# First group's attention by pairs of heads, with all scaling on VectorE, and the rows of sums written later

## The chip, the cores and the metric

The kernel runs on one core of one Trainium2 chip. The time is the device time of an execution in microseconds; 725.45 is the median of three runs (725.28 to 726.31). The engines are PE (matrix products), DVE (VectorE), ACT (ScalarE), POOL (GpSimd) and SP (SyncE, which issues most of the loads here); each works through its own instructions in a fixed order.

## What is computed

An attention with a forgetting bias, then two MLPs in a row, all in fp32:

```python
scores = q @ k.T / sqrt(D)                       # B=2, H=8, S=576, D=64
cum = cumsum(maximum(s, 0), -1)
bias = minimum(-(cum[..., :, None] - cum[..., None, :]), 0)
scores = where(causal, -1e9, scores + bias)
attn = exp(scores - max) ; attn = attn / (sum(attn) + 1e-9)
x = (attn @ v)                                   # 1152 tokens x 512
g = elu(x @ w_in) ; x = g @ w_out                # 512 -> 2048 -> 512
p = probs / (sum(probs) + 1e-9)                  # 4 experts, all of them for every token
out = sum_e p[:, e] * (relu(x @ w1[e]) @ w2[e])  # 512 -> 1024 -> 512
```

## The kernel before

The 1152 tokens are taken in three groups (256, 448, 448). Each group goes through attention, layer 1 (the ELU MLP, 16 units of 128 hidden columns, `layer1` at L648) and layer 2 (the experts, 32 units). The attention of the second group runs in pieces between the products of the first group's MLPs (`Background`, L583); the third group's does so in the second's. Only the first group's attention, `attention_first` (L236), has the core to itself, and it is what the change touches.

The weights of layer 1 come as 64-bit words, 512 KB for a half unit, and are decoded on the chip: two passes on ACT (L146, L148) and two on DVE (L149, L151) for a half (`decode_halves`, L131); each finished unit is also written back (`w_dec`, L154, on POOL's queue) for the later groups. The coded halves lie in tiles that have another use later: wu, gt (3), yh, yl, raw (3), xa (3), ox (3), and around again. A tile is refilled by SP (L127) once its last half has been decoded: the three xa halves are refilled together when the third one's L151 is done, and so for ox. SP works in order, so whatever waits there holds up what is behind: after the refills come the loads of the second group's q, k and v (L370, L372, into a tile named pt; L392 and further) and the weights of layer 2 (`fetch`, L93).

`DEC` says how many halves are decoded at four places within `attention_first`, and `AHEAD` how many are to be decoded at each unit of layer 1: 2n + 8 in `advance` (L573).

`attention_first` as it stands: the products of q and k of all heads into six PSUM banks (L277), then the bias for all of them (L283, L285; the sums enter as high and low parts, `cump` and `cumm`, L262 and L263), then the reductions with the mask on DVE (L295) and the exps on ACT (L297), bank by bank. `normalise` (L299) works on four heads at a time: the first query chunk's 128 columns are scaled on DVE (L305), the second's 256 on ACT (L304). Then three transposes a head (L312), a copy to SBUF (L313), the values (L320) and a copy into `xf` (L322), which layer 1 reads. A unit of layer 1 has its up products (L676), exp and its second pass on ACT (L680, L683), gt on DVE (L684) and its down products (L663).

`cum_sums` (L188) forms the sums along the sequence. `cum_parts` (L194) writes what the later groups read: two rows of ones and, twice, the sums' high part (ACT, L202) and low part (DVE, L203) through one tile named rows, from ACT's own queue (L199, L205), into `rows_d` in HBM. As there is one rows tile, ACT's second L202 waits until the first write has landed. The second group's first item reads `rows_d` into qb and kl (L424, L425).

Of the kernel before, what the change touches and what calls it, by code (L numbers as in the profile page):

```python
# [45 lines left out]
DEC = [2, 5, 8, 10]  # L46
AHEAD = 8
# [4 lines left out]
def tile_kernel(ctx, tc, qT, kT, v, s, w64, w, probs, out):  # L52
# [26 lines left out]
    def ps_att():  # L79
        return ps("att", 2)  # L80
# [155 lines left out]
    def attention_first(x):  # L236
# [23 lines left out]
        for t, sign in ((parts, 1.0), (less, -1.0)):  # L260
# [7 lines left out]
        banks = [(range(0, H, 2), 0, "acc0"), (range(1, H, 2), 0, "acc1"),  # L268
                 ((0, 2), 1, "acc2"), ((1, 3), 1, "acc3"), ((4, 6), 1, "up"), ((5, 7), 1, "up")]
        scores = []  # L270
        for heads, i, tag in banks:
            d0, d1 = 128 * i, 128 * i + 128
            o = ps(tag, 2 if tag == "up" else 1)[:, :len(heads) * d1]
            scores.append(o.rearrange("p (h k) -> p h k", k=d1))
            for n_, h in enumerate(heads):
                r = slice(64 * (h % 2), 64 * (h % 2) + 64)
                PE.matmul(scores[-1][:, n_], qkv[r, 0, h // 2, d0:d1], qkv[r, 1, h // 2, 0:d1],  # L277
                          start=n_ == 0, stop=False, skip_group_check=True)
        for (heads, i, tag), o in zip(banks, scores):
            d0, d1 = 128 * i, 128 * i + 128  # L280
            for n_, h in enumerate(heads):
                one = ones[:, h:h + 1]
                PE.matmul(o[:, n_], one.to_broadcast([80, 128]), parts[:, 0:d1],  # L283
                          start=False, stop=False, skip_group_check=True)
                PE.matmul(o[:, n_], less[:, d0:d1], one.to_broadcast([80, d1]),  # L285
                          start=False, stop=n_ == len(heads) - 1, skip_group_check=True)
        cum_parts()

        def probabilities(bank):
            heads, i, _ = banks[bank]  # L290
            d0, d1 = 128 * i, 128 * i + 128
            for n_, h in enumerate(heads):
                p = pp[h][:, d0:d0 + d1]
                nm = sb([128, 1], "nm", 8)
                DVE.tensor_tensor_reduce(p, scores[bank][:, n_], mask[:, S - d1:], -1.0 / SC,  # L295
                                         3.0e38, ALU.add, ALU.min, nm)
                ACT.activation(p, p, AF.Exp, bias=nm, scale=-1.0, accum_out=sm[:, i, h:h + 1])  # L297

        def normalise(h0):  # L299
            r = sm[:, :, h0:h0 + 4]  # L300
# [7 lines left out]
        def transposes(h):  # L308
            pt = ps_att()
            for m in range(3):  # L310
                ms = slice(128 * m, 128 * m + 128)
                PE.transpose(pt[:, ms], pp[h][:, ms], ident)  # L312
            ACT.activation(ptt[:, h], pt[:, :384], AF.Copy)  # L313

        def values(hp, tag):
            o = ps(tag, 1)
# [5 lines left out]
            ACT.activation(x[:, hp], o[:, :n], AF.Copy)  # L322

        probabilities(0)
        probabilities(1)
        decode_halves(DEC[0])
        probabilities(2)
        probabilities(3)
        normalise(0)
        decode_halves(DEC[1])  # L330
        probabilities(4)
        probabilities(5)
        for h in range(4):
            transposes(h)
        normalise(4)
        values(0, "acc0")
        values(1, "acc1")
        decode_halves(DEC[2])
        for h in range(4, 8):
            transposes(h)  # L340
        decode_halves(DEC[3])
        values(2, "acc2")
        values(3, "acc3")
# [361 lines left out]
    attention_first(x_first)  # L705
    cum_columns(0, 4)
    cum_columns(1, 4)
# [17 lines left out]
    yacc = layer1(0, x_first, background)  # L725
# [321 lines left out]
```

## Time and profile before

| | |
|---|---|
| median of three runs | 725.45 us |
| the profiled execution | 726.64 us |
| its span, first to last instruction | 724.8 us |
| PE busy | 693.3 us, 96% of the span |
| DVE busy | 559.1 us, 77% |
| ACT busy | 371.7 us, 51% |
| mean granted PE clock | 0.985 of full speed |

All times below are from the span's start. A row of the timeline has the start, the time from its first to its last end, the engine, the line, the operation with the tile written, an arrow, and the tiles read; in brackets stands how long the engine had been idle and what released it. A row with an engine's name and q (SPq, ACTq) is an instruction that issues a DMA, not the transfer itself.

### The profile page before, as it was taken

The numbers are of one execution on the slowest core, as the hardware profiler recorded it, in microseconds if no ns is written. First come the engines' busy times: TensorE is split into PE (matmuls) and PEld (weight loads), VectorE is DVE, ScalarE is ACT, GpSimd is POOL, SyncE is SP. The second block draws the span as 40 slices with busy tenths as digits, with TensorE's granted clock in tenths as the row PEclk, the third lists the DMA queues.
The fourth block names the chain that finished last, engine by engine and source line by source line (L and its number), as shares of the span: only waits on it lengthen the run. The fifth ranks groups of instructions, "written<-read, shape, count | busy, mean of one in ns | idle before, by whom it ended". The sixth has DMA issues, their size and how long they took to land.

```text
span 724.8 us, 10238 instructions
## 1 busy us (share of the span) xinstructions
PE 693.3 (96%) x3626; PEld 591.7 (82%) x3626; DVE 559.1 (77%) x1142; ACT 371.7 (51%) x777; POOL 13.6 (2%) x33
## 2 busy tenths in 40 slices
PE   5489789999999999999999999999999999999997
PEld 4378678888878888778899988888888888888886
DVE  4678659988875998886795549988888887887765
ACT  3978658776765878666744333222222222332320
POOL 2011000000000000000000000000000000000000
PEclk9599999999999999999999999999999999999999
DMA  8769994667556453441552000111111111111002
GB/s 325 301 237 368 327 319 160 207 198 216 167 188 203 166 158 108 145 141 59 213 222 88 30 0 1 59 58 59 59 58 59 59 58 59 58 59 59 0 1 101
DMA packets 41954, 96.98 MB, mean 134 GB/s; under 512 B 5200, under 2 KB 18704, under 8 KB 41904
## 3 DMA queue, kind: packets, MB, share of 16 engines
q1 hardware_dynamic: 39440, 87.69, 36.5%
q0 software_dynamic: 2304, 8.39, 2.9%
q8 instruction: 28, 0.46, 0.3%
q10 hardware_dynamic: 160, 0.26, 0.1%
q14 instruction: 22, 0.18, 0.1%
HBM read 85.32 MB, written 11.01 MB: 133 GB/s over the span
## 4 chain that ended last, share of the span: by engine, by line
PE 87%; ACT 4%; DMA 3%; DVE 3%; SPq 2%; issue 1%; DVEq 0%; ACTq 0%
PE acc L562 38%; PE up L562 16%; PE att L882 11%; PE up L882 8%; PE att L517 3%; PE att L490 3%; PE acc L663 2%; PE up L676 2%; PE att L445 1%; PE att L438 1%; SPq L370 1%; PE att L440 1%; DMA wu<-in_w 1%; DMA raw<-in_w 1%; DMA q<-in_qT 1%
## 5 line engine op out<-in xcount | busy, mean ns | idle before, releaser
L562 PE MATMUL acc<-w,h 128*128 128x512 f32 x672 | 172.0, 392 | 0.0
L562 PEld LDWEIGHTS acc<-w,h 128*128 128x128 f32 x672 | 126.1, 188 | 23.0 <-ACT h L892 0.2
L83 DVE TENSOR_TENSOR wu<-raw,wu 128x1024 fp32r<-128x1024 f32 x64 | 78.2, 1222 | 22.9 <-ACT wu L99 21.7
L562 PE MATMUL acc<-gt,wu 128*128 128x448 f32 x384 | 88.6, 373 | 0.0
L630 DVE SCALAR_TENSOR_TENSOR ox<-acc,pr,ox 128x512 f32<-128x512 f32 x105 | 78.6, 748 | 10.7 <-PE acc L562 8.6
L892 ACT ACTIVATE h<-c 128x448 fp32r<-128x448 f32 x48 | 27.4, 574 | 114.7 <-DVE c L898 114.7
L99 ACT ACTIVATE wu<-raw 128x1024 fp32r<-128x1024 f32 x64 | 67.5, 1055 | 22.4 <-PE acc L562 16.5
L562 PEld LDWEIGHTS acc<-gt,wu 128*128 128x128 f32 x384 | 70.1, 188 | 8.7 <-issue 2.6
L882 PE MATMUL att<-S,top 128*128 128x448 f32 x288 | 66.3, 365 | 0.0
L882 PEld LDWEIGHTS att<-S,top 128*128 128x128 f32 x288 | 54.0, 188 | 6.7 <-issue 0.2
L562 PE MATMUL acc<-wu,gt 128*128 128x512 f32 x192 | 56.4, 409 | 0.0
L562 PE MATMUL up<-yh,wu 128*128 128x256 f32 x256 | 52.6, 287 | 0.0
L893 DVE SCALAR_TENSOR_TENSOR h<-c,h 128x448 fp32r<-128x448 f32 x48 | 29.9, 624 | 18.7 <-ACT h L892 18.7
L882 PE MATMUL up<-x2a,top 128*128 128x448 f32 x192 | 44.2, 366 | 0.0
L562 PEld LDWEIGHTS up<-yh,wu 128*128 128x128 f32 x256 | 41.9, 190 | 2.7 <-issue 1.7
L562 PE MATMUL up<-xa,wu 128*128 128x448 f32 x192 | 43.6, 371 | 0.0
L562 PE MATMUL up<-ox,wu 128*128 128x448 f32 x192 | 42.1, 368 | 0.7 <-DVE e L688 0.7
L480 ACT ACTIVATE p<-p,nm 128x384 f32<-128x384 f32 (+4 forms) x56 | 34.5, 617 | 13.6 <-DVE nm L475 13.4
L680 ACT ACTIVATE e<-up 128x448 f32<-128x448 f32 (+1 forms) x48 | 23.5, 490 | 33.7 <-PE up L562 31.7
L882 PEld LDWEIGHTS up<-x2a,top 128*128 128x128 f32 x192 | 35.9, 188 | 4.8 <-ACT p L907 0.5
L562 PEld LDWEIGHTS up<-ox,wu 128*128 128x128 f32 x192 | 36.0, 188 | 4.6 <-DVE e L688 1.1
L892 ACT ACTIVATE h<-up 128x448 fp32r<-128x448 f32 x16 | 8.8, 547 | 58.1 <-PE up L882 58.1
(186 smaller groups left out, 1217.8 us busy)
## 6 DMA issues: line engine op xcount, KB each, us to landing
raw<-in_w SPq DMA_DIRECT2D x41, 512.0 KB
raw<-w_dec SPq DMA_DIRECT2D x32, 512.0 KB
raw<-in_w SPq DMA_DIRECT2D x16, 1024.0 KB
w_dec<-wu POOLq DMA_DIRECT2D x16, 512.0 KB, 6.7
k<-in_kT SPq DMA_DIRECT2D x16, 288.0 KB
xa<-in_w SPq DMA_DIRECT2D x6, 512.0 KB
ox<-in_w SPq DMA_DIRECT2D x6, 512.0 KB
cbp<-cum_d SPq DMA_DIRECT2D x16, 144.0 KB
```

Of the source, the lines that this page charges most:

```text
L83: DVE.tensor_tensor(out=lo, in0=x, in1=hi.bitcast(F32), op=ALU.subtract)
L99: ACT.activation(t[:, 0], x, AF.Copy)
L480: ACT.activation(p, p, AF.Exp, bias=nm, scale=-1.0, accum_out=sm)
L490: PE.transpose(pt[:cb[c + 1] - cb[c], m, :], p[:, cb[c]:cb[c + 1]], ident)
L517: PE.matmul(o[64 * j:64 * j + 64, qs:nq], job["v"][:n, c, 64 * j:64 * j + 64], job["pt"][:n, j, c, qs:nq], start=c == 0, stop=c == n_c - 1)
L562: PE.matmul(o, a[m], b[n], start=first and i == 0, stop=last and i == 2)
L630: DVE.scalar_tensor_tensor(out=o_sb, in0=o, scalar=pr[:, i, e:e + 1], in1=o_sb, op0=ALU.mult, op1=ALU.add)
L663: PE.matmul(o, t[:, 512 + 128 * c:640 + 128 * c], gt, start=k == 0, stop=k == NAB - 1)
L680: ACT.activation(e, o, AF.Exp)
L882: PE.matmul(bank, tops[q][:, m, op, cs], x[:, n, c], start=first and c + i == 0, stop=c == 1 and i == 2, skip_group_check=True)
L892: ACT.activation(h[:, 0, u, cs], c, AF.Relu)
L893: DVE.scalar_tensor_tensor(out=h[:, 1, u, cs], in0=c, scalar=0.0, in1=h[:, 0, u, cs].bitcast(F32), op0=ALU.max, op1=ALU.subtract)
```

## The change

In the first group's attention:

- The loads of q and k are split into two chunk pairs each, four DMAs in place of two; the first coded half, then v, then the other halves follow. `cum_sums` is written behind them.
- PE makes twelve 128x128 products whose result nothing reads (`keep_warm`), ahead of the first product of q and k.
- The work goes by pairs of heads: products and bias of one pair, both query chunks of a head in one bank, then reductions and exps, scaling, transposes and values of that pair, with the next pair's steps in between.
- `normalise` makes all sixteen scalings on DVE; ACT has none.
- `DEC` and `AHEAD` are smaller: four halves are decoded within the attention instead of ten, and 2n + 6 by unit n.

`cum_parts`, with the write of `cum_d`, and `cum_columns` move from the attention into a hook after unit k = 3 of layer 1.

```diff
-DEC = [2, 5, 8, 10]
-AHEAD = 8
+DEC = [1, 2, 3, 4]
+AHEAD = 6
...
     def cum_sums():
-        SP.dma_start(out=s_sb, in_=s)
         ACT.activation(s_sb, s_sb, AF.Relu, scale=SC)
         DVE.tensor_tensor_scan(cum, s_sb, s_sb, 0.0, ALU.add, ALU.bypass)
+    def cum_parts():
+
         ACT.dma_start(out=cum_d, in_=cum)
-
-    def cum_parts():
-
         one = sb([B * H, S], "bias", 2)
...
-        cum_sums()
-        SP.dma_start(out=qkv[:, 0], in_=qT[0, :, 0:n].rearrange("(c p) n -> p c n", p=128))
-        SP.dma_start(out=qkv[:, 1], in_=kT[0, :, 0:n].rearrange("(c p) n -> p c n", p=128))
-        fetch_halves(2)
+        SP.dma_start(out=s_sb, in_=s)
+        for c in (0, 2):
+            for i, t in enumerate((qT, kT)):
+                SP.dma_start(out=qkv[:, i, c:c + 2], in_=t[0, 128 * c:128 * c + 256, 0:n]
+                             .rearrange("(c p) n -> p c n", p=128))
+        fetch_halves(1)
...
+        cum_sums()
...
+        chunks = [(0, 128), (128, 256)]
+        banks = {}
+
+        def scores(hp):
+            for j in range(2):
+                h = 2 * hp + j
+                banks[h] = ps(f"acc{h % 4}", 1) if h < 4 or h > 5 else ps("up", 2)
+            for d0, d1 in chunks:
+                for j in range(2):
+                    r = slice(64 * j, 64 * j + 64)
+                    PE.matmul(banks[2 * hp + j][:, d0:d0 + d1], qkv[r, 0, hp, d0:d1],
+                              qkv[r, 1, hp, 0:d1], start=d0 == 0, stop=False,
+                              skip_group_check=True)
...
-            for h in range(h0, h0 + 4):
-                ACT.activation(pp[h][:, 128:], pp[h][:, 128:], AF.Copy, scale=sm[:, 1, h:h + 1])
-                DVE.tensor_scalar(pp[h][:, :128], pp[h][:, :128], sm[:, 0, h:h + 1], None,
-                                  op0=ALU.mult)
...
+            for h in (2 * hp, 2 * hp + 1):
+                for i, (d0, d1) in enumerate(chunks):
+                    p = pp[h][:, d0:d0 + d1]
+                    scaled = DVE.tensor_scalar(p, p, sm[:, i, h:h + 1], None, op0=ALU.mult)
+            return scaled
...
+        def keep_warm(products):
+
+
+            o = ps_att()[:, :128]
+            for _ in range(products):
+                last = PE.matmul(o, ident, ident, start=True, stop=True)
+            return last
+
+        with tc.issue_after(keep_warm(12).ins):
+            for hp in range(3):
+                scores(hp)
         probabilities(0)
+        decode_halves(DEC[0])
+        scores(3)
         probabilities(1)
-        decode_halves(DEC[0])
+        normalise(0)
+        transposes(0)
         probabilities(2)
...
+    def sums_hook(k):
+        if k == 3:
+            with tc.issue_after(after[0].ins), tc.issue_after(after[1].ins):
+                cum_parts()
+            cum_columns(0, 4)
+            cum_columns(1, 4)
+
+    yacc = layer1(0, x_first, background, sums_hook)
```

How this moves the instructions, at three places. First DVE, at the start of the attention; z is half a decoded half, k_, acc_ and sm_ are the probabilities, the banks and the sums, and "ISA" rows of L295 or L299 are the reductions. Before:

```order
L203 SCALAR_TENSOR_TENSOR rows<-cum,rows 16x576
L263 SCALAR_TENSOR_TENSOR cump<-cum,cump 16x256
L263 SCALAR_TENSOR_TENSOR cumm<-cum,cumm 16x256
L203 SCALAR_TENSOR_TENSOR rows<-cum,rows 16x576
L149 SCALAR_TENSOR_TENSOR wu<-wu,z_251 128x512
L151 SCALAR_TENSOR_TENSOR wu<-wu 128x512
L295 ISA k_137,nm<-acc_154,mask 128x128
L295 ISA nm 128x1
```

and now:

```order
L264 SCALAR_TENSOR_TENSOR cump<-cum,cump 16x256
L264 SCALAR_TENSOR_TENSOR cumm<-cum,cumm 16x256
L299 ISA k_138,nm<-acc_168,mask 128x128
L299 ISA nm 128x1
L299 ISA k_138,nm<-acc_168,mask 128x256
```

The low halves of the rows (L203) and the first decoded half stood ahead of the first reduction; now the first reduction follows `cumm` directly.

Second SP, at the first refills of xa and ox; the names after "waits" are counters of landed DMAs and of the engines. Before:

```order
L127 DMA raw<-in_w 128x1024 [waits DMAHW3_49,DVE_49,Activation_49]
L127 DMA xa<-in_w 128x1024 [waits DMAHW4_49,DVE_49,Activation_49]
L127 DMA xa<-in_w 128x1024 [waits DMAHW5_49]
L127 DMA xa<-in_w 128x1024 [waits DMAHW6_49]
L127 DMA ox<-in_w 128x1024 [waits DMAHW7_49,DVE_49,Activation_49]
L127 DMA ox<-in_w 128x1024 [waits DMAHW0_49]
```

and now, from the last raw refill:

```order
L127 DMA raw<-in_w 128x1024 [waits DMAHW7_49,DVE_49,Activation_49]
L127 DMA xa<-in_w 128x1024 [waits DMAHW1_49,DMAHW0_49,DMAHW2_49,DVE_49,Activation_49]
L127 DMA xa<-in_w 128x1024 [waits DMAHW2_49]
L127 DMA xa<-in_w 128x1024 [waits DMAHW3_49]
L444 DMA kl<-rows_d 4x128 [waits DMAHW6_49,DMAHW5_49,DMAHW0_49]
L444 DMA kl<-rows_d 4x128
L443 DMA qb<-rows_d 4x128 [waits DMAHW7_49,DMAHW4_49]
L127 DMA ox<-in_w 128x1024 [waits DVE_49,Activation_49]
L127 DMA ox<-in_w 128x1024 [waits DMAHW1_49]
```

The ox refill followed the xa refill; now the reads of `rows_d` for the second group's first item (kl, kl, qb) stand between them, and qb waits for DMAHW4, which the second rows write on ACT's queue counts up.

Third ACT and DVE, at the new place of the rows. ACT now, from the first of the two copies to the pass behind the second (before, both stood ahead of the attention's exps):

```order
L200 ACTIVATE rows<-cum 16x576
L699 ACTIVATE e<-up 128x256 [waits PE_49]
L148 ACTIVATE z_531<-xa 128x512 [waits DVE_49]
L702 ACTIVATE e<-e 128x256 [waits Activation_49]
L146 ACTIVATE wu<-xa 128x512
L203 DMA rows_d<-rows 16x1152 [waits DMAHW0_49,DVE_49]
L146 ACTIVATE wu<-ox 128x512 [waits DMAHW3_49]
L148 ACTIVATE z_541<-ox 128x512
L699 ACTIVATE e<-up 128x256 [waits PE_49]
L148 ACTIVATE z_560<-ox 128x512 [waits DMAHW4_49,DVE_49]
L200 ACTIVATE rows<-cum 16x576 [waits DMAHW0_49]
L702 ACTIVATE e<-e 128x256 [waits Activation_49]
```

The second copy (L200) waits for DMAHW0, the landing of the first write (L203), and the second pass of a unit's e (L702) is behind it. DVE now, around the same unit:

```order
L151 SCALAR_TENSOR_TENSOR wu<-xa,wu 128x512 x2
L201 SCALAR_TENSOR_TENSOR rows<-cum,rows 16x576
L703 SCALAR_TENSOR_TENSOR gt<-up,e 128x256
L149 SCALAR_TENSOR_TENSOR wu<-wu,z_531 128x512
L151 SCALAR_TENSOR_TENSOR wu<-xa,wu 128x512
L149 SCALAR_TENSOR_TENSOR wu<-wu,z_541 128x512
L151 SCALAR_TENSOR_TENSOR wu<-ox,wu 128x512
L201 SCALAR_TENSOR_TENSOR rows<-cum,rows 16x576
L703 SCALAR_TENSOR_TENSOR gt<-up,e 128x256
```

Before, the third xa half (the last of these three L151 with xa) stood ahead of the gt of the fifth unit:

```order
L151 SCALAR_TENSOR_TENSOR wu<-xa,wu 128x512
L149 SCALAR_TENSOR_TENSOR wu<-wu,z_506 128x512
L151 SCALAR_TENSOR_TENSOR wu<-ox,wu 128x512
L684 SCALAR_TENSOR_TENSOR gt<-up,e 128x256
L149 SCALAR_TENSOR_TENSOR wu<-wu,z_496 128x512
L151 SCALAR_TENSOR_TENSOR wu<-xa,wu 128x512
L149 SCALAR_TENSOR_TENSOR wu<-wu,z_532 128x512
L151 SCALAR_TENSOR_TENSOR wu<-ox,wu 128x512
L684 SCALAR_TENSOR_TENSOR gt<-up,e 128x256
```

Its place is now behind that gt (the first of the two L703 in the rows of the change).

## Rows read from the trace of the kernel before

**Rows 1.** The page: busy time of each engine, and the chain by engine.
```profile
PE 693.3 (96%) x3626; PEld 591.7 (82%) x3626; DVE 559.1 (77%) x1142; ACT 371.7 (51%) x777; POOL 13.6 (2%) x33
...
PE 87%; ACT 4%; DMA 3%; DVE 3%; SPq 2%; issue 1%; DVEq 0%; ACTq 0%
```

**Rows 2.** Windows: length, busy us (PE, PEld, DVE, ACT, POOL), clock, DMA share, GB/s.
```profile
25.00:30.00 5.00, 0.92 (x5) 0.52 (x5) 3.90 (x9) 5.00 (x16) 1.16 (x2) 0.50 1.01 361
45.00:50.00 5.00, 5.00 (x25) 4.41 (x24) 2.47 (x4) 3.00 (x6) 0.53 (x1) 1.00 0.57 227
65.00:70.00 5.00, 5.00 (x25) 4.41 (x24) 4.32 (x9) 4.41 (x9) 0.53 (x1) 1.00 1.03 418
80.00:90.00 10.00, 7.57 (x27) 6.39 (x28) 7.30 (x15) 8.55 (x21) 1.06 (x2) 0.83 1.08 298
100.00:110.00 10.00, 9.10 (x53) 7.77 (x54) 7.56 (x27) 7.42 (x22) 0.00 (x0) 1.00 0.89 260
```

**Rows 3.** Timeline of PE: up products of the third, twelfth, thirteenth unit.
```profile
43.88 1.99 PE L676 MATMUL up<-xf,wu 128*128 128x256 f32 x8 [1.55 <-DVE gt L684]
...
75.06 1.89 PE L676 MATMUL up<-xf,wu 128*128 128x256 f32 x8
...
82.43 3.68 PE L676 MATMUL up<-xf,wu 128*128 128x256 f32 x8 [3.76 <-DVE gt L684]
```

**Rows 4.** Timeline: SP's refills, DVE's gt of the fifth unit, ACT's qb.
```profile
53.14 1.28 SPq L127 DMA_DIRECT2D xa<-in_w  x3
...
55.00 0.42 DVE L684 SCALAR_TENSOR_TENSOR gt<-up,e 128x256 f32<-128x256 f32 x1
...
56.81 1.32 SPq L127 DMA_DIRECT2D ox<-in_w  x3
...
80.84 0.31 ACT L429 ACTIVATE qb<-pt 64x128 fp32r<-64x128 f32 x1 [5.21 <-DMA pt<-in_qT]
```

**Rows 5.** Timeline of ACT and DVE from the first half to the first reduction.
```profile
8.43 0.67 ACT L148 ACTIVATE z<-wu 128x512 int32<-128x512 uint32 x1 [2.73 <-DMA wu<-in_w]
...
9.77 0.41 DVE L263 SCALAR_TENSOR_TENSOR cumm<-cum,cumm 16x256 fp32r<-16x256 f32 x1
...
13.16 0.68 ACT L202 ACTIVATE rows<-cum 16x576 fp32r<-16x576 f32 x1 [3.46 <-DMA rows_d<-rows]
...
13.87 0.74 DVE L203 SCALAR_TENSOR_TENSOR rows<-cum,rows 16x576 fp32r<-16x576 f32 x1 [3.69 <-ACT rows L202]
...
15.72 0.69 DVE L151 SCALAR_TENSOR_TENSOR wu<-wu 128x512 int32<-128x512 int32 x1
16.33 0.28 DVE L295 CUSTOM_DVE_ANT_0 k<-acc,mask 128x128 f32<-128x128 f32 x1
```

**Rows 6.** Groups of ACT by line and form, 10 to 60 us.
```profile
L313 ACT ACTIVATE pt<-att 128x384 f32<-128x384 f32 x8 | 3.6, 507 | 0.0
...
L297 ACT ACTIVATE k<-k,nm 128x256 f32<-128x256 f32 x6 | 3.0, 493 | 0.0
...
L304 ACT ACTIVATE k<-k,sm 128x256 f32<-128x256 f32 x6 | 2.6, 502 | 0.0
...
L297 ACT ACTIVATE k<-k,nm 128x128 f32<-128x128 f32 x6 | 2.3, 388 | 1.7 <-DVE nm L295 1.7
...
L322 ACT ACTIVATE xf<-acc 128x256 f32<-128x256 f32 x4 | 1.5, 419 | 0.0
```

**Rows 7.** Chain in order of time: the first rows write; the first raw weights.
```profile
8.43 4.70 DMA rows_d<-rows
...
86.50 5.80 DMA raw<-in_w
```

**Rows 8.** Timeline of the start: the load of s and its reader.
```profile
0.75 0.40 SPq L189 DMA_DIRECT2D bias<-in_s  x1
...
2.53 0.68 ACT L190 ACTIVATE bias<-bias 16x576 f32<-16x576 f32 x1 [0.50 <-DMA bias<-in_s]
```

**Rows 9.** The page, DMA issues: the write-backs of decoded weights.
```profile
w_dec<-wu POOLq DMA_DIRECT2D x16, 512.0 KB, 6.7
```

More of the change, by code (lines that the diff above doesn't have):

```diff
@@ L264, in attention_first @@
                                      in1=t[:B * H].bitcast(F32), op0=ALU.mult, op1=ALU.subtract)
[L268 to L278, printed above, removed]
@@ L279, in attention_first @@
-        for (heads, i, tag), o in zip(banks, scores):
-            d0, d1 = 128 * i, 128 * i + 128
-            for n_, h in enumerate(heads):
-                one = ones[:, h:h + 1]
[L283 to L297, printed above, removed]
@@ L299, in normalise @@
-        def normalise(h0):
-            r = sm[:, :, h0:h0 + 4]
+        chunks = [(0, 128), (128, 256)]
[10 more added lines that the diff above has]
+                              skip_group_check=True)
+            for j in range(2):
+                h = 2 * hp + j
+                one = ones[:, h:h + 1]
+                for d0, d1 in chunks:
+                    o = banks[h][:, d0:d0 + d1]
+                    PE.matmul(o, one.to_broadcast([80, 128]), parts[:, 0:d1],
+                              start=False, stop=False, skip_group_check=True)
+                    PE.matmul(o, less[:, d0:d1], one.to_broadcast([80, d1]),
+                              start=False, stop=d0 > 0, skip_group_check=True)
@@ new lines, in probabilities @@
+        def probabilities(hp):
+            for j in range(2):
+                h = 2 * hp + j
+                for i, (d0, d1) in enumerate(chunks):
+                    p = pp[h][:, d0:d0 + d1]
+                    nm = sb([128, 1], "nm", 8)
+                    DVE.tensor_tensor_reduce(p, banks[h][:, d0:d0 + d1], mask[:, S - d1:],
+                                             -1.0 / SC, 3.0e38, ALU.add, ALU.min, nm)
+                    ACT.activation(p, p, AF.Exp, bias=nm, scale=-1.0, accum_out=sm[:, i, h:h + 1])
@@ L301, in normalise @@
+        def normalise(hp):
+            r = sm[:, :, 2 * hp:2 * hp + 2]
             DVE.tensor_scalar(r, r, 1e-9, None, op0=ALU.add)
             DVE.reciprocal(r, r)
-            for h in range(h0, h0 + 4):
-                ACT.activation(pp[h][:, 128:], pp[h][:, 128:], AF.Copy, scale=sm[:, 1, h:h + 1])
-                DVE.tensor_scalar(pp[h][:, :128], pp[h][:, :128], sm[:, 0, h:h + 1], None,
-                                  op0=ALU.mult)
[L308 to L313, printed above, removed]
@@ L315, in values, with transposes @@
-        def values(hp, tag):
-            o = ps(tag, 1)
+            for h in (2 * hp, 2 * hp + 1):
+                for i, (d0, d1) in enumerate(chunks):
+                    p = pp[h][:, d0:d0 + d1]
+                    scaled = DVE.tensor_scalar(p, p, sm[:, i, h:h + 1], None, op0=ALU.mult)
+            return scaled
+        def transposes(hp):
+            for h in (2 * hp, 2 * hp + 1):
+                pt = ps_att()
+                for m in range(3):
+                    ms = slice(128 * m, 128 * m + 128)
+                    PE.transpose(pt[:, ms], pp[h][:, ms], ident)
+                ACT.activation(ptt[:, h], pt[:, :384], AF.Copy)
@@ L317, in values @@
+        def values(hp):
+            o = ps(f"acc{(hp + 2) % 4}", 1)
             for c, q0 in ((0, 0), (1, 128)):
@@ L321, in values @@
                               ptt[:, h, 256 * c:256 + 128 * c], start=c == 0, stop=c == 1)
-            ACT.activation(x[:, hp], o[:, :n], AF.Copy)
+            return ACT.activation(x[:, hp], o[:, :n], AF.Copy)
+        def keep_warm(products):
[6 more added lines that the diff above has]
+                scores(hp)
         probabilities(0)
+        decode_halves(DEC[0])
+        scores(3)
         probabilities(1)
-        decode_halves(DEC[0])
+        normalise(0)
+        transposes(0)
         probabilities(2)
+        normalise(1)
+        transposes(1)
+        values(0)
+        decode_halves(DEC[1])
         probabilities(3)
[L329 to L337, printed above, removed]
+        normalise(2)
+        transposes(2)
+        values(1)
         decode_halves(DEC[2])
-        for h in range(4, 8):
-            transposes(h)
+        last = [normalise(3)]
+        transposes(3)
+        values(2)
+        last.append(values(3))
         decode_halves(DEC[3])
-        values(2, "acc2")
-        values(3, "acc3")
+        return last
     def attention_parts(g, x):
@@ L704, in tile_kernel @@
     x_first = sb([128, NCC, GROUPS[0][1]], "xf", 1)
-    attention_first(x_first)
-    cum_columns(0, 4)
-    cum_columns(1, 4)
+    after = attention_first(x_first)
     xs = [None, None, None]
```

1 line of the change is left out of this document (removed).

## Prediction

> **What bounds the kernel now.** The page first: PE is busy for 693.3 us, 96% of the span, and 87% of the chain of waits is PE [rows 1]. So only stretches where PE stands still can give anything. The windows find them: 0.92 of 5 us in 25 to 30, then 7.57 of 10 in 80 to 90 and 9.10 of 10 in 100 to 110 [rows 2]; afterwards PE is the bound. There are thus two holes: the first group's attention, and the end of its layer 1. A gain in the first reaches the end only if it is still there after the second.
>
> The first hole is ACT and DVE work. The third up product, the first after which PE runs on without a break, starts at 43.88, and the twelfth at 75.06: nine steps of 3.46 us [rows 3]. The second hole is a wait for data: ACT stands 5.21 us at the qb copy until pt<-in_qT has landed at 80.84, and the thirteenth up product starts at 82.43, after 3.76 us of PE idle and at half pace, 3.68 us for what takes 1.89 [rows 3, 4]. The clock of that stretch is 0.83 [rows 2]. Those transfers come late because the stream of transfers is full: 418 GB/s from 65 to 70 us [rows 2]. SP started refilling at 53.14, when the third xa half had been decoded, and sent the ox refill at 56.81 [rows 4]. So the question is less when the attention ends than when SP starts this stream.
>
> **The front, part by part.** (1) DVE's first reduction starts at 16.33, though its last needed input, cumm, is written from 9.77 to 10.18. Between lie a copy that waits 3.46 us for the landing of the first rows write, its DVE half (0.74 us) and the first decoded half [rows 5]. In the change the reductions stand directly behind cumm. SP's two extra loads, at 0.40 each [rows 8], push half 0 back by 0.8, but nothing of the reductions waits for it any more. First reduction about 10.2 to 11, 5.5 us earlier.
>
> (2) ACT sets the pace from there. What it must still do before the third up product: eight exps at 0.39 and eight at 0.49, 7.0; eight pt copies, 3.6; four xf copies, 1.5 [rows 6]; four coded halves at two passes of 0.67 [rows 5], 5.4; about four passes for the first two units, at the 0.42 of the gt pass of the same width [rows 4], 1.7: 19.2, so 10.9 plus that is about 30 at the earliest. Gone are eight scalings at 0.43 [rows 6] and six coded halves, 3.4 and 8.0 us. DVE takes eight scalings of 128x256 more; at the same 0.42 that is 3.4 us, beside ACT's work, with DVE at 3.90 of 5 and ACT at 5.00 [rows 2]. If pairs overlap badly, each of four pays a bare turn through PE, DVE and ACT of about 1.9 (six transposes, one copy, four scalings, from the pieces above): 37.5. I take **33.5**, 10.4 earlier than 43.88, nearer the floor because the next pair's exps fill most turns.
>
> (3) Twelve unread products: a 128x256 product costs 1.99/8, 0.25 us [rows 3], one of half the width 0.12 to 0.25 by clock, all of them 1.5 to 3.0 us, before q and k land, when PE has nothing to read. Without that cover, at most 3.0 on the front, which the stream hides.
>
> **The stream.** In the old trace 11.1 us pass from the third up product to the gt of the fifth unit at 55.00 [rows 3, 4]. In the new order the third xa half is finished behind this gt, in the old one ahead of it. So 33.5 + 11.1 = 44.6; two rows copies on ACT at 0.68 and two halves on DVE at 0.74 [rows 5], half of it under other waits, 1.4; the decoding pair of 0.69 each behind gt, 1.4; some wait, 0.6 (here lie the issues of the cum_d and bias writes and the column copies, which move to this place too): xa refill at **48.0**, against 53.14: **-5.1**.
>
> (4) Then SP meets something new. Ahead of the ox refill stands qb<-rows_d, which waits for the second rows write; that is issued after ACT's second copy, which waits for the landing of the first. On SP everything is queued behind it: ox refill, yh, yl, raw, then q and k of the next group. On ACT it is the second pass of the fifth unit's e: the copy follows four passes, 2.4 us, behind the first write, so ACT stands for w - 2.4, and PE loses that from a lead that it would lose in the second hole anyway. The pr loads, which stood behind qb and kl, now go ahead of them; nobody waits for that. With a write of w us from issue to landing, first issued at about 46, the second has landed at 46 + 2w + 1.4. No row shows w at this place. Below: 1.8, the load of s with an empty stream (issue 0.75, its reader starts at 2.53) [rows 8]. Above: 6.7, the median of the 512 KB write-backs [rows 9]. Nearest: 4.70 for this very write, behind a full stream [rows 7]. In the old trace the stream is busy for 0.57 from 45 to 50 [rows 2], so I take 4.0: 55.4, and 0.4 for SP. The three xa halves would keep the stream fed until 53.8 (2.0 to the first landing, after the 1.8 of an empty stream [rows 8], 3.8 for 1.5 MB at 418 GB/s). So the stream stands empty for **+2.0**; -2.4 at w = 1.8 means none, and 7.4 at 6.7.
>
> The row has 4.70 us for these 72 KB (16 x 1152 values) [rows 7]. The Trainium skill, "DMA: Bandwidth & Descriptors", section "Anatomy of one DMA — SWDGE (gpsimd) path", gives about 2.0 us plus bytes at 436 GB/s for a write issued by GpSimd; estimated from that page the hold would vanish and the sum would be near that of the second case below. The 4.70 speaks against it while the stream is full.
>
> (5) When q and k land, at 77.7 (80.84 - 3.1), some fourteen up products lie behind instead of twelve, since qb stands behind the e of the thirteenth unit in the new order. Two units of 3.46 fewer remain, 6.9. But the rest also hangs on the stream: the first raw weights land at 92.30 [rows 7], later ones further on, and PE still loses 0.90 in 100 to 110 [rows 2]. I keep 1.5 of it, between nothing and 6.9: **-1.5**.
>
> **Sum:** -5.1 + 2.0 - 1.5 = -4.6. The profiled execution took 726.64 us and would take 722.0. It lies 1.2 above the median of 725.45, so the forecast for the median is **720.9**.
>
> **The rivals.** *The rows writes land early* (w near 1.8 to 3), so a hold of at most 0.6, and 2.5 of the 6.9 kept: -5.1 + 0.6 - 2.5 = -7.0, 718.4. For: the 0.57 from 45 to 50 [rows 2]. Against: 4.70 in the only row. Chance 0.23. *The hold eats the gain* (w near 5.5): +5.0 instead of 2.0, and the two units worth nothing: -0.1, 725.3; the front ending at 37 comes to the same. Chance 0.14. *Slower: SP's wait becomes the new head of the stream.* At w = 6.7, 46 + 13.4 + 1.4 + 0.4 = 61.2, against an empty stream from 53.8: +7.4, nothing from the units, -5.1 + 7.4 = +2.3: 727.8; it decides from w about 6.2. For: the 6.7 median, writes behind a full stream. Against: these are a seventh of the bytes. Chance 0.07. *The front isn't shortened*, because half 0's decoding blocks ACT or the pairs run one after the other: 725.5. Against: the order of DVE's rows. Chance 0.02.
>
> **How the numbers follow.** The forecast has 0.54, with 719.2 to 722.6 as its own range (w 3.2 to 4.8 gives 0.4 to 3.6 us of hold). A measurement of this kernel tells about 0.2%, 1.45 us, from no change. Forecast and early writes are both beyond that: 0.77, and some of the third case, 0.03: faster 0.80. Same: 0.13, slower 0.07. The range goes from 717.8, the early writes with 0.6 more of the two units, to 725.0, where the hold has taken nearly all; it leaves out the slow case, part of the third and the far end of the second.
>
> **What would show it.** First reduction at 10 to 11; third up product 31 to 36; xa refill issued at about 48 and ox refill at 54 to 58, with a gap in the transfers between; pt<-in_qT landed at 76 to 79; ACT's wait at qb of some 2 to 5 us still there. I am wrong if the ox refill follows the xa refill at once, if the third up product starts after 38, or if PE stands still after 105 us.

## The result, and the profile after

The changed kernel takes 733.61 us (median of four runs, 732.40 to 736.22) where the kernel before takes 725.37: a ratio of 1.0118 [1.0088, 1.0148]. It is slower by 1.2%; forecast were 720.9 and a range to 725.0. The profiled execution took 733.40, with a span of 731.5.

The page of the kernel after has PE busy for 14 us more than before [rows 1], though it has no more work for it than twelve unread products:

```profile
PE 707.5 (97%) x3650; PEld 600.8 (82%) x3650; DVE 561.2 (77%) x1154; ACT 368.5 (50%) x769; POOL 13.6 (2%) x33
```

Where the time went is read from the windows, by the stages of the forecast: the front, the time of the first refills, the rest of the first group's layer 1, the end of it, and the start of layer 2. Columns as in [rows 2]; the number behind an x counts instructions. Before:

```profile
0.00:30.00 30.00, 11.48 (x72) 10.12 (x73) 17.76 (x61) 19.07 (x55) 6.08 (x19) 0.79 0.94 348
30.00:45.00 15.00, 12.58 (x73) 9.47 (x72) 10.73 (x32) 14.16 (x32) 1.12 (x3) 0.84 0.69 231
45.00:85.00 40.00, 36.24 (x163) 31.40 (x162) 27.10 (x46) 28.40 (x59) 4.57 (x9) 0.97 0.89 317
85.00:105.00 20.00, 17.96 (x83) 14.82 (x81) 13.59 (x36) 12.31 (x34) 1.80 (x4) 0.98 1.05 311
105.00:120.00 15.00, 14.93 (x104) 12.97 (x103) 12.90 (x46) 12.21 (x40) 0.00 (x0) 1.00 0.53 190
0.00:80.84 80.84, 57.74 (x298) 48.89 (x298) 52.94 (x131) 57.50 (x134) 11.46 (x29) 0.89 0.86 314
```

After:

```profile
0.00:30.00 30.00, 24.56 (x110) 18.89 (x111) 13.41 (x59) 14.14 (x43) 4.95 (x17) 0.66 0.90 335
30.00:45.00 15.00, 12.33 (x67) 8.26 (x66) 10.22 (x30) 12.04 (x28) 1.22 (x2) 1.00 0.13 48
45.00:85.00 40.00, 38.98 (x181) 33.90 (x179) 33.44 (x61) 32.12 (x65) 5.85 (x11) 1.00 0.97 361
85.00:105.00 20.00, 14.48 (x58) 11.80 (x56) 10.87 (x26) 11.67 (x32) 1.59 (x3) 0.83 1.01 293
105.00:120.00 15.00, 10.36 (x54) 8.88 (x54) 8.29 (x28) 5.72 (x19) 0.00 (x0) 0.85 0.75 205
65.00:70.00 5.00, 5.00 (x24) 4.38 (x24) 4.92 (x10) 5.00 (x11) 1.06 (x2) 1.00 0.74 220
0.00:80.84 80.84, 71.70 (x335) 57.48 (x336) 55.49 (x147) 56.82 (x131) 11.61 (x30) 0.87 0.79 290
```

(The last row of each is the whole time until q has landed in the kernel before, for later.) From 120 to 720 us both are alike, with PE busy for 599.1 of 600 us. What counts is what PE has done by 120 us, and its busy time doesn't measure that where the clock is low. Four lines differ. **0 to 30**: PE is busy for 24.56 instead of 11.48 us, at a mean clock of 0.66, while ACT and DVE do some 5 and 4 us less. **30 to 45**: 48 GB/s instead of 231; the stream of transfers all but stops. **65 to 70**: it thins out a second time, to 220 GB/s, where before has 418 [rows 2]. **105 to 120**: PE works 10.36 instead of 14.93 us, and at a clock of 0.85. In the row above, 85 to 105, it is also busy for less, but only because the second hole, which ended at 82.43 before [rows 3], now lies in it: by 105 us PE has run 392 instructions without the 24 of the unread products, and 391 before. By 120 us it is 446 against 495. So the loss is made from 105 to 120 us.

**The front.** The timeline of the kernel after, at its start:

```profile
9.84 0.66 ACT L148 ACTIVATE z<-wu 128x512 int32<-128x512 uint32 x1 [6.60 <-DMA wu<-in_w]
...
10.40 0.40 ACT L263 ACTIVATE cump<-cum 16x256 fp32r<-16x256 f32 x1
...
11.30 0.47 PE L288 MATMUL acc<-cump,ones 80*128 80x128 f32 x1 [3.60 <-DVE cump L264]
...
12.68 0.29 DVE L299 CUSTOM_DVE_ANT_0 k<-acc,mask 128x128 f32<-128x128 f32 x1 [1.10 <-PE acc L290]
```

The first reduction is at 12.68, not at 10 to 11, though its neighbours on DVE are as planned. `cump` on ACT stands behind L148, the first pass of the first coded half, and that pass waits 6.60 us for its load. PE meanwhile stands still, with the first q and k landed and multiplied, for 3.60 us. The windows behind that pause show what it does to PE:

```profile
15.00:20.00 5.00, 5.00 (x25) 4.12 (x23) 3.81 (x17) 2.96 (x10) 0.00 (x0) 0.50 1.02 419
20.00:25.00 5.00, 5.00 (x24) 4.12 (x24) 3.76 (x23) 2.42 (x11) 0.00 (x0) 0.50 1.02 419
25.00:30.00 5.00, 5.00 (x19) 2.53 (x18) 1.20 (x6) 2.88 (x9) 0.00 (x0) 0.50 0.83 284
```

PE is busy without a break from 15 to 30 at a granted clock of 0.50, the lower of its two levels (1.2 GHz), with ACT at 2.4 to 3.0 of 5 and DVE at 1.2 to 3.8. So PE's products at the lower clock look like the pace of the front, and not ACT; e2 and e5 below test that. The Trainium skill, "TensorE: Matmul & The Clock Gate", section "What's actually happening", says that throttled is the default state and that activity releases it; in these rows it isn't released through 15 us in which the profile counts PE as busy, so here busy time alone does not tell which level is granted.

**The stream.** The timeline from the third up product to the qb copy, with the refills and the rows writes:

```profile
42.28 1.99 PE L695 MATMUL up<-xf,wu 128*128 128x256 f32 x8 [2.42 <-DVE gt L703]
...
43.50 0.34 SPq L127 DMA_DIRECT2D yh<-in_w  x1
...
53.26 0.41 DVE L703 SCALAR_TENSOR_TENSOR gt<-up,e 128x256 f32<-128x256 f32 x1
...
53.36 0.31 ACTq L203 DMA_DIRECT2D rows_d<-rows  x1
...
55.07 1.63 SPq L127 DMA_DIRECT2D xa<-in_w  x3
...
58.98 0.68 ACT L200 ACTIVATE rows<-cum 16x576 fp32r<-16x576 f32 x1 [3.17 <-DMA rows_d<-rows]
...
60.48 0.31 ACTq L203 DMA_DIRECT2D rows_d<-rows  x1
...
62.74 0.69 DVE L151 SCALAR_TENSOR_TENSOR wu<-ox,wu 128x512 int32<-128x512 int32 x1
...
64.88 0.24 SPq L443 DMA_DIRECT2D qb<-rows_d  x1
...
65.22 1.30 SPq L127 DMA_DIRECT2D ox<-in_w  x3
...
88.76 0.31 ACT L448 ACTIVATE qb<-pt 64x128 fp32r<-64x128 f32 x1 [6.06 <-DMA pt<-in_qT]
```

The third up product starts at 42.28, 1.6 earlier than before [rows 3], not 10.4. The first refill of all (yh) follows at 43.50; the first one before (yl) was at 35.81:

```profile
35.81 0.35 SPq L127 DMA_DIRECT2D yl<-in_w  x1
```

The xa refill is at 55.07, behind the raw refills, and ox at 65.22, 10.15 later, with `qb<-rows_d` straight ahead of it. Before, 3.67 us lay between the two [rows 4]. SP's hold at qb is the smaller part of this: the third ox half is decoded only at 63.43 (62.74 and 0.69), and without its L151 the refill couldn't go out, so SP's hold is 1.8 us at most. The larger part is on ACT. Its second copy stands 3.17 us until the first rows write has landed, and the passes of the last ox halves are behind it. The third ox half's L151 starts 8.4 us after the third xa half's (54.30); before it was 3.7 (52.38 and 56.05).

ACT has q at 88.76 instead of 80.84, after a wait of 6.06. The chain of waits goes from the landing of the first rows write through ACT's passes, decoding for the most part, to the load of q, and from there through ACT and SP to two later loads:

```profile
53.36 5.60 DMA rows_d<-rows
...
72.02 16.72 DMA pt<-in_qT
...
98.33 8.53 DMA v<-in_v
...
107.93 5.85 DMA raw<-in_w
```

PE's second hole is still there, but it costs nothing against before, since two more units of layer 1 lie ahead of it. The fifteenth up product and the first product of layer 2 after:

```profile
89.88 3.78 PE L695 MATMUL up<-xf,wu 128*128 128x256 f32 x8 [4.61 <-DVE gt L703]
...
103.27 0.47 PE L581 MATMUL up<-yh,wu 128*128 128x256 f32 x1
```

Before, they were at 91.13 and at 104.95:

```profile
104.95 0.47 PE L562 MATMUL up<-yh,wu 128*128 128x256 f32 x1
```

PE pays behind that. Its waits from 100 to 120 us, in total, times and longest:

```profile
PE up L581 <- DVE yl L83: 2.0, 1, 2.0
PE att L459 <- DMA qb<-rows_d: 1.9, 1, 1.9
PE up L581 <- ACT wu L99: 1.3, 1, 1.3
```

All three go back to loads that stand behind q in SP's queue. yl is the low half of layer 1's output; DVE comes to it late, since it stands at L229 for the load of `cbp`:

```profile
105.22 0.49 DVE L229 TENSOR_SCALAR bias<-cbp,cum_p 128x512 f32<-128x512 f32 x1 [2.02 <-DMA cbp<-cum_d]
```

L99 waits for the raw weights issued at 107.93; the third load of raw weights for layer 2 before was at 101.64. So q's landing is where the lateness of SP's queue can be read, 7.9 us, and PE feels it some 15 us later.

### The profile page after: what moved, and what is told of

The parts are those of the page before. It is cut to its first block, busy times and chain, and to the rows that moved or that the text cites. A ratio compares the mean times of both kernels' runs of the same rounds, so it can differ in the third digit from the quotient of the medians.

```text
span 731.5 us, 10289 instructions
## 1 busy us (share of the span) xinstructions
PE 707.5 (97%) x3650; PEld 600.8 (82%) x3650; DVE 561.2 (77%) x1154; ACT 368.5 (50%) x769; POOL 13.6 (2%) x33
## 4 chain that ended last, share of the span: by engine, by line
PE 85%; DMA 6%; ACT 3%; DVE 3%; issue 1%; SPq 1%; ACTq 0%; DVEq 0%
PE acc L581 37%; PE up L581 16%; PE att L907 10%; PE up L907 8%; PE att L536 3%; PE att L509 3%; DMA pt<-in_qT 2%; PE att L464 1%; PE att L457 1%; DMA v<-in_v 1%; PE att L459 1%; ACT wu L146 1%; DMA wu<-in_w 1%; PE acc L326 1%; DMA raw<-in_w 1%
## 5 line engine op out<-in xcount | busy, mean ns | idle before, releaser
L99 ACT ACTIVATE wu<-raw 128x1024 fp32r<-128x1024 f32 x64 | 67.5, 1055 | 20.4 <-PE acc L581 13.6
L581 PE MATMUL up<-yh,wu 128*128 128x256 f32 x256 | 55.0, 295 | 1.3 <-ACT wu L99 1.3
L581 PEld LDWEIGHTS up<-yh,wu 128*128 128x128 f32 x256 | 43.4, 196 | 4.5 <-issue 1.8
L695 PE MATMUL up<-xf,wu 128*128 128x256 f32 x128 | 33.3, 401 | 8.3 <-DVE gt L703 8.1
L581 PE MATMUL up<-yl,wu 128*128 128x256 f32 x128 | 37.4, 292 | 2.0 <-DVE yl L83 2.0
```

Of the source, the lines that this page charges most:

```text
L99: ACT.activation(t[:, 0], x, AF.Copy)
L581: PE.matmul(o, a[m], b[n], start=first and i == 0, stop=last and i == 2)
L695: PE.matmul(o, t[:, dm(c)], x[:, c], start=c == 0, stop=c == NCC - 1)
```

## The experiments

The expectations use letters. **H**: SP's hold behind the rows writes makes the loss. **D** (S in later runs): the halves left out of the front do, because they are decoded later, their tiles are refilled later, and the stream runs empty between 30 and 45 us. **C** (with C1 and C2): the slow start of the front does, by the late `cump` and PE's half clock. All runs in one table: starts from each trace (third up product, first refill, ox refill, and ACT's qb copy, when q has landed), then the rate of transfers from 30 to 45 us and from 0 until q has landed:

| kernel | ratio to before | third up | first refill | ox refill | q landed | GB/s 30 to 45 | GB/s 0 to q |
|---|---|---|---|---|---|---|---|
| before | 1 | 43.88 | 35.81 | 56.81 | 80.84 | 231 | 314 |
| after | 1.0118 [1.0088, 1.0148] | 42.28 | 43.50 | 65.22 | 88.76 | 48 | 297 |
| e1 | 1.0075 [1.0050, 1.0101] | 41.17 | 42.40 | 63.70 | 88.86 | 69 | 298 |
| e2 | 0.9987 [0.9971, 1.0003] | 42.34 | 34.85 | 56.47 | 80.17 | 265 | 321 |
| e3 | 1.0019 [0.9997, 1.0040] | 35.19 | 36.41 | 60.46 | 84.46 | 170 | 312 |
| e4 | 1.0037 [1.0017, 1.0057] | 40.36 | 41.58 | 57.82 | 83.22 | 115 | 310 |
| e5 | 1.0049 [1.0030, 1.0069] | 37.73 | 38.95 | 60.99 | 85.63 | 130 | 310 |
| e6 | 0.9999 [0.9978, 1.0020] | 38.33 | 38.95 | 55.22 | 81.09 | 121 | 320 |
| e7 | 0.9923 [0.9895, 0.9950] | 36.27 | 28.51 | 52.67 | 76.11 | 307 | 337 |
| e8 | 0.9967 [0.9946, 0.9989] | 36.42 | 28.48 | 52.90 | 76.49 | 303 | 336 |
| e9 | 1.0110 [1.0086, 1.0135] | 42.84 | 44.07 | 64.04 | 90.41 | 38 | 286 |
| e10 | 0.9937 [0.9913, 0.9961] | 35.22 | 29.13 | 52.00 | 75.61 | 330 | 344 |
| e11 | 1.0135 [1.0112, 1.0157] | 41.47 | 43.96 | 67.34 | 90.64 | 45 | 292 |
| e12 | 0.9914 [0.9896, 0.9932] | 35.59 | 29.27 | 52.07 | 74.83 | 319 | 343 |

Diffs are against the kernel after, except that of e6.

### e1: the first item's loads out of SP's way

```diff
-            split(items[0])
+                split(items[0])
```

The line moves into the `with late()` around it: qb and kl of the second group's first item are then read behind the last load of coded weights.

> The changed kernel with the first item's qb and kl reads put behind the last coded load, so that SP waits for no rows write ahead of the ox refill; ACT still waits for the first write. Theory H (SP's hold at qb made the change slow: ox refill 10.15 us behind xa refill, 3.67 before): ox refill about 4 us behind xa refill, pt<-in_qT lands near 82.5 instead of 88.7, time about 728. Theory D (too few halves are decoded in the front, so the refills come late whatever SP waits for): the ox refill comes at most 2 us earlier, time 731 to 733. Theory C (the front's half clock): ox as in H, but the front unchanged, 729 to 731.

No reads of `rows_d` stand ahead of the ox refill any more, yet it is issued at 63.70, 8.15 behind xa: SP waits for DVE's L151 there (6.8 us the longest), since the third ox half is decoded no sooner (62.95). ACT's stand at the second copy is still there, with 2.91. q lands at 88.86, as in the kernel after. The ratio is 0.43 points lower, with intervals that overlap. SP's hold is not the main cause; the other part of the rows writes' price, ACT's stand, is not tested by this run.

### e2: the old amounts of decoding

```diff
-DEC = [1, 2, 3, 4]
-AHEAD = 6
+DEC = [2, 5, 8, 10]
+AHEAD = 8
```

> The changed kernel with the old numbers of halves decoded (2, 5, 8, 10 in the attention, 2n+8 behind it). Theory D: the empty stream from 31 to 46 us shrinks, first refill near 37 instead of 43.5, xa refill near 50, time 727 to 729. Theory H: the hold moves along with the xa refill, so the time falls by the shift of the refill at most, 730. Theory C: ACT has idle time in a front that PE at half clock sets, so ten halves cost little there; third up product 43 to 46, time as in D.

The loss is gone: 0.9987. The timeline of e2:

```profile
10.99 0.40 ACT L263 ACTIVATE cump<-cum 16x256 fp32r<-16x256 f32 x1
...
42.34 1.99 PE L695 MATMUL up<-xf,wu 128*128 128x256 f32 x8 [1.76 <-DVE gt L703]
```

The late `cump` (10.99) and the third up product (42.34) are as in the kernel after. Six more halves are decoded in the front, and it isn't any longer for them: ACT and DVE had that much time left beside a slow PE. The first refill is 8.65 earlier, q lands 8.59 earlier. The ox refill is 4.79 behind xa: with more halves decoded by each unit, all ox passes but one stand ahead of ACT's second copy, which waits for nothing here. The slow start and the later rows then cost nothing against before as long as the halves aren't left out.

### e3: the first pair's exps ahead of the decoding

```diff
-        probabilities(0)
-        decode_halves(DEC[0])
+        first = probabilities(0).ins
+        with tc.issue_after(first):
+            decode_halves(DEC[0])
...
-        decode_halves(DEC[1])
+        with tc.issue_after(first):
+            decode_halves(DEC[1])
```

`probabilities` returns its last exp. This takes L148 from ahead of `cump`; the amounts stay small.

> The changed kernel with the decoding of the first two coded halves put behind the first pair's exps on ACT, so that cump and cumm don't wait for the first half to land. Theory C: cump starts near 4.7 instead of 10.4, the bias products follow q and k without a gap, the clock stays full after the unread products, first reduction near 8.5, third up product 33 to 36 instead of 42.3, time 725 to 728. Theory D: the decoding is no earlier, so the refills move by 2 us at most, time 731 to 733. Theory H: the hold stays at 10 us between xa and ox refill, time falls by what the xa refill gains.

The front comes out as the forecast had it, better at its start and 1.7 later at its end. The timeline of e3:

```profile
8.36 0.29 DVE L299 CUSTOM_DVE_ANT_0 k<-acc,mask 128x128 f32<-128x128 f32 x1 [1.77 <-PE acc L290]
...
48.73 0.31 ACTq L203 DMA_DIRECT2D rows_d<-rows  x1
...
50.43 1.53 SPq L127 DMA_DIRECT2D xa<-in_w  x3
...
53.40 0.68 ACT L200 ACTIVATE rows<-cum 16x576 fp32r<-16x576 f32 x1 [2.24 <-DMA rows_d<-rows]
...
54.90 0.31 ACTq L203 DMA_DIRECT2D rows_d<-rows  x1
...
60.12 0.24 SPq L446 DMA_DIRECT2D qb<-rows_d  x1
...
60.46 1.66 SPq L127 DMA_DIRECT2D ox<-in_w  x3
```

PE has the full clock from 10 to 20 (1.00 and 0.98 in the windows). Yet the time is that of before, 1.0019. So a right front does not make the forecast's gain: from the third up product to the xa refill it takes 15.24 (14.5 in the forecast), the first rows write lands in 4.67, the second in 5.22 (4.0 in the forecast, for both), and ox goes out 10.03 behind xa (7.8). The third ox half is decoded at 57.85 here, so SP's hold is 2.6 of that.

### e4: the rows of sums back in the front

```diff
+        cum_parts()
         probabilities(0)
...
     def sums_hook(k):
         if k == 3:
-            with tc.issue_after(after[0].ins), tc.issue_after(after[1].ins):
-                cum_parts()
```

> The changed kernel with the rows written in the front as before, everything else as changed. Theory H: ox refill about 4 us behind xa refill, pt<-in_qT near 82 to 84, time about 728, less what ACT's wait of 4 to 5 us for the first rows write costs the front. Theory D: the refills still wait for decoding, 732 to 735. Theory C: the front gets later still, third up product 44 to 47, time 732 to 736.

The ox refill goes out 3.22 behind xa, 7.4 earlier than in the kernel after, and the loss falls to 0.37%. The third up product comes 1.9 earlier too, and the first refill with it, but of that only 0.5 is left at the xa refill (54.60). So nearly all that ox gains comes from the place of the rows. The run puts that place, with the 1.9 us of the front, at some 0.8 points beside the small amounts and the late `cump`.

Taking back any one of the three thus takes away most of the loss of 1.18 points: the amounts (e2) 1.31, the late `cump` (e3) 0.99, the place of the rows (e4) 0.81. All three work on the same refill, ox at 65.22, which then comes at 56.47, 60.46 and 57.82. Together they come to far more than the loss, so no share of it can be given to each.

### e5: 29 unread products instead of 12

```diff
-        with tc.issue_after(keep_warm(12).ins):
+        with tc.issue_after(keep_warm(29).ins):
```

> The changed kernel with 29 unread products in place of 12, nothing else: they last until cump is ready (about 10.5 us), so PE doesn't stand still ahead of the bias products. Theory C1 (the front is slow because PE's pause of 3.6 us takes the clock to half, where it stays until 30 us): clock 1.00 from 5 to 25, all products of the four pairs done by 18 to 20 instead of 24, third up product 36 to 38 instead of 42.3, time 728 to 730 on the scale of 733.6. Theory C2 (only the late cump counts, the clock nothing): third up product 41 to 43, time 733.

PE then has 0.42 us of pause ahead of the bias products in place of 3.60, though `cump` (9.96) is hardly earlier. The windows of e5:

```profile
10.00:15.00 5.00, 4.97 (x40) 3.51 (x40) 2.46 (x13) 3.64 (x13) 0.00 (x0) 1.00 1.03 420
20.00:25.00 5.00, 4.83 (x20) 2.83 (x20) 2.99 (x17) 3.32 (x12) 0.00 (x0) 0.50 1.02 416
```

The clock is 1.00 in the stretch where the kernel after has 0.50, and the third up product comes 4.55 earlier. So the pause and the half clock behind it made at most 4.6 of the front's delay (`cump` is 0.4 earlier as well); with e3, which also has `cump` early, it is 7.1. Both runs keep the small amounts of decoding, and both stay above before.

### e6: the small amounts in the kernel before

```diff
-DEC = [2, 5, 8, 10]
-AHEAD = 8
+DEC = [1, 2, 3, 4]
+AHEAD = 6
```

> The kernel before with the changed kernel's numbers of decoded halves (1, 2, 3, 4 and 2n+6), nothing else. Theory D (the end follows how early the halves are decoded and the tiles refilled): the front gets shorter, third up product 35 to 39 instead of 43.9, but the first refill comes at 38 to 41 instead of 35.8 and the stream of transfers has a hole of 8 us or more; xa refill 54 to 57, time 728 to 731 against 725.4. If the front alone sets the end: 720 to 723.

No difference: 0.9999. The same edit that costs 1.3 points in the changed kernel costs nothing here. In the kernel before ACT is busy for 5.00 of 5 in the front [rows 2], so halves left out shorten it: the third up product comes at 38.33, 5.55 earlier, and the first refill only 3.1 later. In the changed kernel ACT doesn't set the pace, and nothing is shortened. A second difference isn't separated from this one: in the kernel before the rows are written in the front, and ox goes out 3.79 behind xa in e6. The 121 GB/s from 30 to 45 us are made up again: from 0 until q has landed, e6 has 320 GB/s and the kernel before 314. The second gap of the kernel after, 220 GB/s from 65 to 70, isn't there in e6, with 419.

### e7: e3 and e2 together

> The changed kernel with both: the first halves' decoding behind the first pair's exps, and 2, 5, 8, 10 halves with 2n+8. Theories C and D both hold and add: third up product 37 to 40, first refill near 30, xa refill near 46, ox refill 50 to 54 behind the rows write, pt<-in_qT lands 74 to 77, time 719 to 722. If the stream was full anyway by then: 724 to 726.

Faster than both kernels: 0.9923, which is some 719.8 us on the scale on which before has 725.4. The windows of e7, to set beside the first two rows of the tables at the top:

```profile
0.00:30.00 30.00, 24.48 (x148) 19.19 (x150) 21.53 (x78) 22.97 (x64) 6.14 (x19) 0.89 0.94 349
30.00:45.00 15.00, 11.61 (x50) 9.48 (x50) 10.19 (x29) 10.13 (x23) 1.60 (x3) 0.89 0.88 307
```

The front has ACT at 22.97 of 30 and the stream runs on at 307 GB/s. PE works 14.93 of 15 us from 105 to 120, as before. With e2, e3 and the kernel after this makes a square: ten halves instead of four give 1.3 points with a late `cump` (1.0118 to 0.9987) and 1.0 with an early one (1.0019 to 0.9923); an early `cump` gives 1.0 and 0.6. Within the intervals these two add up, nearly. The six more halves move the third up product from 35.19 (e3) to 36.27, by 1.1.

### e8, e10: SP's hold taken out of e7

e8 is e7 with the edit of e1. e10 is e7 with two rows tiles, so that the second copy doesn't wait for the first write:

```diff
-            t = sb([B * H, 2, S], "rows", 1, F32R)
+            t = sb([B * H, 2, S], "rows", 2, F32R)
```

> The kernel of the run before with qb and kl of the first item also read behind the last coded load. Theory H for what is left of the hold: 1 to 3 us less than the run before, 717 to 720. If the hold is gone with the earlier rows: the same within 1 us.

> The fastest so far (first halves behind the first exps, 2, 5, 8, 10 halves) with two rows tiles. Theory H: ox refill near 50 instead of 52.7, 1 to 2 us faster, 719 to 720 on the scale of 725.4 for before. Theory S (the stream is already busy for 0.95 from 30 to 85 us): no gain, 720 to 722.

Neither gains: 0.9967 and 0.9937 against 0.9923. In e7 `qb<-rows_d` isn't ahead of the ox refill any more, which goes out 5.23 behind xa. In e8 the first products of layer 2 start at 99.19 instead of 95.78, with q landed as in e7; what holds them was not followed.

### e9: two rows tiles in the kernel after

The edit of e10 alone.

> The changed kernel with two rows tiles, so that the second rows write and its two halves don't wait for the first write to land; SP reads qb and kl ahead of the xa refill. Theory H (each rows write of about 5 us stands one after the other ahead of the refills): ox refill near 60 instead of 65.2, no wait of ACT at the second copy, time 728 to 731 instead of 733.6. Theory S (what counts is the empty stream from 30 to 46 us, which is the same here): time within 1.5 of 733.

No difference, 1.0110. The scheduler also moved the reads of `rows_d`: e9 has them (60.51) ahead of the xa refill, which is now at 62.19, and not of ox. So the hold was moved more than removed, and the run says little of its price.

### e11: the second chunk scaled on ACT

```diff
-                    scaled = DVE.tensor_scalar(p, p, sm[:, i, h:h + 1], None, op0=ALU.mult)
+                    if i:
+                        ACT.activation(p, p, AF.Copy, scale=sm[:, i, h:h + 1])
+                    else:
+                        scaled = DVE.tensor_scalar(p, p, sm[:, i, h:h + 1], None, op0=ALU.mult)
```

> The changed kernel with the second query chunk scaled on ACT as before, the rest as changed. If the move of the scaling matters: the front gets 2 to 4 us later by eight passes of 0.43 on ACT, time 735 to 737. If PE's half clock sets the front, in which ACT is busy for less than 4 of 5 us: third up product 42 to 44, time within 1.5 of 733.

1.0135 against 1.0118, with overlapping intervals: where the scaling stands makes no difference that these runs can tell.

### e12: e7 without the unread products

```diff
-        with tc.issue_after(keep_warm(12).ins):
-            for hp in range(3):
-                scores(hp)
+        for hp in range(3):
+            scores(hp)
```

> The fastest so far without the twelve unread products. Theory C1 (the clock of the front comes from these products): PE at half clock through the first products of q and k, clock full only from about 10 to 11 us, bias products at half pace, first reduction 9 to 10 instead of 8.0, third up product 2 to 4 us later, time 722 to 725. If they don't matter: 721.

0.9914: the products are worth nothing once `cump` is early. The first reduction is later (10.06 against 8.03 in e7), the third up product is 0.7 earlier and q lands 1.3 earlier. e12 and e7 are the best of these kernels, not to be told apart.

## Why the prediction was wrong

The forecast had the third up product at 33.5; it came at 42.28. That front is the step that failed, by two readings of it, and the sum had no term for what the halves left out do to the stream. Its frame held: the end follows SP's queue. The column "q landed" goes from 74.83 (e12, 0.9914) to 90.64 (e11, 1.0135): 15.8 us of landing for 0.0221 x 725.4 = 16.0 us of time, and all fourteen kernels lie within 2.6 us of a line of 1 us for 1 us through the kernel before. And q lands 22.8 to 26.4 us behind the ox refill in all of them.

- **"nothing of the reductions waits for it any more"**, in part (1), said of half 0, was wrong. On DVE it is so; on ACT the half's L148 stands ahead of `cump`, which the bias products wait for, and waits for a load itself. The order of one engine's rows was read, and not the other's. With it came the pause of PE and the half clock (e3, e5): 42.28 where 33.5 was forecast. One rival named this step, "half 0's decoding blocks ACT", with a chance of 0.02 and no loss; what stood against it was again the order of DVE's rows.
- **"ACT sets the pace from there"**, in part (2), was wrong. The six halves left out were booked as 8.0 us gained on ACT. In the kernel after, ACT is busy for about half of 15 to 30 us; e2 decodes all ten halves and starts the third up product at 42.34 instead of 42.28. The 8.0 were worth nothing there, and 1.1 with the early `cump` (e7 against e3). PE's score and bias products, which are the pace at half clock, had no term at all. Two counts were off besides. The sum has four halves on ACT ahead of the third up product; the trace has six to seven (L146 six times, L148 seven), since 2n + 6 asks for six and eight at the first two units. And 1.99/8 is half of a 128x256 product in fp32: the row counts eight for four products. The twelve unread products took 5.00 us in place of 1.5 to 3.0, and still ended as the first q and k landed.
- **The stream** was summed from the xa refill on, as if all ahead of it were as before. Halves decoded later are refilled later: the first refill moved from 35.81 to 43.50. What that does is seen from the rates until q has landed: time by rate gives 25.4 MB before (80.84 x 314) and 26.4 MB after (88.76 x 297), and between 25.4 and 26.6 MB in all fourteen kernels. So q comes when about so many bytes have been moved, and each stretch in which the stream stands empty and that isn't made up delays it. From 30 to 45 us 183 GB/s fewer for 15 us are 2.7 MB, or 6.6 us at the 418 GB/s of a full stream [rows 2]. From 65 to 70 us another 1.0 MB are missing, around the late ox refill; a gap there is what the forecast looked for. Between the two the stream makes up a part. At 80.84 us the kernel after has moved 1.9 MB less than before, and it moves 1.0 MB more ahead of q, which was not followed: 2.9 MB, 7.0 us at 418 GB/s, for the 7.9 by which q is late. The sum had -5.1 for the xa refill and no term for this.
- **The hold** in part (4) has the right mechanism and the wrong size: landings of 5.60 and 4.40 (60.48 to 64.88) in the kernel after, 4.67 and 5.22 in e3, for a w of 4.0. With w near 5 and a right front the forecast's own sum comes close to its second case, no gain, and e3 measured that, 1.0019. It also put ACT's stand at the second copy at nothing, as PE's lead would be lost anyway. But the decoding of the last ox halves stands behind that copy, and the ox refill with it: 8.4 us from the third xa half to the third ox half in place of 3.7, against 1.8 at most for SP's own hold. e4, without either, has 3.2.
- **Right**: 11.0 us from the third up product to the gt of the fifth unit (53.26), for 11.1; ACT's wait at qb still there, with 6.06 for 2 to 5. In part (5), fourteen up products lie ahead of q's landing instead of twelve: the fourteenth starts at 81.66, and the first product of layer 2 comes 1.7 earlier than before in spite of the late q. What it gave was lost again behind it, by the later loads, so the 1.5 kept of it can't be seen in the time.

Two of the signs named for being wrong were there: a third up product after 38, and PE standing still after 105 us.

The range was too narrow because all its cases shared the front at 33.5 (or 37) and the stream ahead of xa. The slower rival was there, with 727.8 and for another reason, SP's wait alone.

## What to carry to other kernels

Work left out of a stage is worth its time only if the engine that does it sets the pace there, after the change as well; otherwise it only moves, and whatever its end releases (here refills of tiles, and so the transfers behind them) moves with it. When a change defers work, follow the first buffer that comes free later, and not only the one that the sum begins with. And read the new order on every engine that a chain passes through: one early pass that waits for a load, or one copy that waits for a landing, holds up all that is behind it on its engine. Last, a late landing is a mark: the place of the loss is where the engine that bounds the kernel has done less, here 15 us behind q.

## What the runs showed of the hardware

PE was granted 0.50 from 15 to 30 us while busy for 5.00 of 5, after a pause of 3.60, with score and bias products of 64 and 80 rows and then transposes and values; e5, with 0.42 of pause at the same place, had 1.00 from 10 to 15 and fell to 0.50 from 20 to 25 at 4.83 of 5. In e3, at a clock of 1.00, the same first bias product (128x128) took 0.33 where the kernel after has 0.47, and one weight load 0.18 to 0.19 instead of 0.29 to 0.33, so the small products pay for the lower level in both.

A write of 72 KB took 4.4 to 5.6 us from issue to release of its reader in the kernel after and in e3, with the stream at 412 GB/s from 55 to 65 us in the kernel after.
